# Conversion steps, warming matmuls, the order list of the attention rounds, and GpSimd for one part of a token mix

## The chip, the cores and the metric

The kernel runs on one core of a Trainium2 chip. TensorE (PE) multiplies matrices, VectorE (DVE), ScalarE (ACT) and GpSimd (POOL) work on tiles, and SyncE (SP) issues the DMAs. Each engine takes its instructions from a queue of its own, in order, and semaphores make one engine wait for another. The metric is the device time of one execution in microseconds (us); less is better.

## The reference, cut to what matters

Three blocks stand behind each other. Only their shapes matter here: two batches, 12 heads, 448 tokens, 64 numbers per head, 768 = 12 x 64 model columns, 1024 hidden columns.

```python
scores = scale * np.matmul(q, k.transpose(0, 1, 3, 2))       # causal mask, then softmax
x = softmax(scores) @ v                                      # heads joined: 768 columns
xk = mu_k * x + (1.0 - mu_k) * x_prev                        # x_prev: the token before
xr = mu_r * x + (1.0 - mu_r) * x_prev
x2 = sigmoid(xr @ w_r) * (np.maximum(xk @ w_k, 0.0) ** 2 @ w_v)
h = np.maximum(x2 @ w_in, 0.0)
out = (h * sigmoid(conv(h, conv_w)) @ w_out)
```

The weights arrive as 64-bit floating point numbers, so the kernel has to turn them into 32-bit ones itself.

## The kernel before

**Attention.** There are 12 jobs, one for each batch and pair of heads, numbered 0 to 11. The loop at L450 runs rounds i = -1 to 14. In each round the table `ORDER` (L426) names the operations of several jobs in the order in which every engine gets them: `n` is the next job (its transposes `kqT`, their copies `kqH` and `kqL`, its first scores `sc`), `c` the job of this round (more scores, `red` for the row maximum on DVE, `exp` on ACT), `l` the last one (`norm` on GpSimd, transposes `T` on PE, copies `C`), `p` the one before (`V`, the product with v on PE, and `out`), `a` the one before that (`mixP`, `mixD`, `mixH`, `mixL`). Within the rounds PE, ACT, DVE and GpSimd follow this order by hand; around them a scheduler has placed the instructions, so some matmuls of the next block already stand between the last rounds' work.

**Token mixes.** For each 128 columns c and batch b a mix has four steps: scale the token before (`mix_p`), add the scaled token (`mix_d`, L343, DVE), write the rounded high part (`mix_h`), and write the rest (`mix_l`, a subtraction at L78). Kind 1 makes xr inside the rounds with GpSimd for all but `mix_d`. Kind 0 makes xk behind the rounds: scaling and high part on ACT, `mix_d` and the subtraction on DVE.

**Matrix products.** Every fp32 product is made of three matmuls (`mm3`, L63 to 66): high by high (L64), high by low (L65), low by high (L66). The blocks are called by their banks: `pr` = xr @ w_r (6 weight slices, 216 matmuls), `pk` (8 slices), `pv`, `ph` and `pout`.

**Weight conversion.** A slice of weights (`wr0` to `wr5`, then `wk0` and so on) goes through seven steps, each taken by one call of `step()` (L407): one `Abs` on ACT (L100), four operations on DVE (L102, L104, L106, L108), the high part on ACT (`wr0hl`, L74), the low part on DVE (`wr0hl`, L78). In the rounds `c.w.0` to `c.w.2` take three steps per job from job 4 on, 24 in all; two more follow behind the loop (L465). `take()` finishes what is missing when a product needs the slice.

**Warming matmuls.** `keep_warm(n)` (L443) issues n matmuls whose result nobody reads: 12 ahead of everything and three behind every `kqT`, `sc` and `T` of the rounds i = -1, 0 and 1, in all 69.

Of the kernel before, what the change touches and what calls it, by code (L numbers as in the profile page):

```python
# [19 lines left out]
def kernel(  # L20
# [39 lines left out]
    def f32(ap):  # L60
        return ap.bitcast(F32)
# [49 lines left out]
    def load(w, m, name, rows):  # L111

        if rows:
            kt, n = 1, w.shape[1]
            src = w[m * P:(m + 1) * P, :].rearrange("p (k f) -> p k f", k=1)
        else:
            kt, n = w.shape[0] // P, P
            src = w[:, m * P:(m + 1) * P].rearrange("(k p) f -> p k f", p=P)
        raw = wp.tile([P, NF * P], I64, tag="wraw", name=f"{name}{m}raw")

        in_order(
            nc.sync.dma_start(out=raw[:, :kt * n].rearrange("p (k f) -> p k f", k=kt), in_=src)
        )
        return raw, kt * n, f"{name}{m}"
# [82 lines left out]
    class Job:  # L207
# [4 lines left out]
            self.done = 0  # L212

        def load(self, first=False):
            for src, n in ((k, "k"), (q, "q"), (v, "v")):
                t = rawp.tile([CP, NQ, 2, D], F32, tag=n, name=f"r{n}_{self.n}", bufs=4 if n == "v" else 2)
                for j in range(2):
                    dma = nc.sync.dma_start(
                        out=t[:, :, j],
                        in_=src[self.b, 2 * self.hp + j].rearrange("(c p) d -> p c d", p=CP),  # L220
                    )
                    if first:
                        tc.keep_in_program_order(dma)
                self.raw[n] = t
# [33 lines left out]
        def red(self, c, j):  # L258

            w, i = (c + 1) * CP, 2 * c + j  # L260
            self.s[c, j] = s_sb = sp.tile([CP, S], F32, tag="s", name=f"s_{self.n}_{i}", bufs=3)
            nc.vector.tensor_tensor_reduce(  # L262
                s_sb[:, :w], self.scs[c][j][:CP, :w], maskw[:, S - w:], -SCALE, 3e38,
                ALU.add, ALU.min, self.st[:, 0, i:i + 1],
            )

        def exp(self, c, j):
            w, i = (c + 1) * CP, 2 * c + j
            self.p[j, c] = p = sp.tile([CP, w], F32, tag=f"p{c}{j}", name=f"p_{self.n}_{i}", bufs=2)
# [54 lines left out]
        def mixL(self):  # L324
            mix_l(1, xr[self.hp], self.b, self.hp)

        def w(self, _):
            if self.i >= 4:
                step()

    ms = {}
# [14 lines left out]
        split_h("p" if kind else "s", dst[:, 0, TOK[b]], ms[kind, b, c])  # L346

    def mix_l(kind, dst, b, c):
        split_l("p" if kind else "v", dst[:, 1, TOK[b]], ms[kind, b, c], dst[:, 0, TOK[b]])

    def mix(kind, dst, b, c):
        mix_p(kind, b, c)
        mix_d(kind, b, c)
        mix_h(kind, dst, b, c)
        mix_l(kind, dst, b, c)

    TOK = [slice(b * S, (b + 1) * S) for b in range(B)]
# [61 lines left out]
    def take():
# [4 lines left out]


    ORDER = """  # L426
        c.w.0 c.exp.0.1 l.rec.2.4 l.norm.1.1 p.T.3 c.sc.3 p.C.1 p.C.0 c.exp.0.0 a.mixP p.T.2 l.norm.1.0
        c.red.1.1 n.kqT.q c.red.1.0 p.C.3 c.w.1 a.mixD n.kqT.k c.sc.2 c.red.3.0 l.norm.3.1 c.exp.1.1
        c.red.3.1 p.C.2 p.V.0 l.norm.2.0 n.kqH.q n.kqH.k n.kqL.q p.V.2 c.exp.1.0 l.norm.2.1 l.norm.3.0
        c.exp.3.0 p.V.3 n.kqL.k p.V.1 c.exp.3.1 c.red.2.1 l.norm.0.0 l.T.4 n.sc.0 c.red.2.0 c.rec.0.2 n.sc.1  # L430
        c.w.2 c.exp.2.1 a.mixH a.mixL l.T.1 p.out l.T.0 c.norm.0.1 l.C.4 n.red.0.1 c.exp.2.0 n.red.0.0
    """
    ROUNDS_AGO = {"n": -1, "c": 0, "l": 1, "p": 2, "a": 3}
    order = [x.split(".") for x in ORDER.split()]
# [8 lines left out]
    def keep_warm(n):  # L443
        for _ in range(n):
            nc.tensor.matmul(warm[:, :P], ident, ident, start=True, stop=True)  # L445

    keep_warm(12)
    ET = mybir.EngineType
    with tc.manual_schedule(engines={ET.PE, ET.Activation, ET.DVE, ET.Pool}):
        for i in range(-1, B * NPAIR + 3):  # L450
            if 2 <= i + 2 < B * NPAIR:
                jobs.append(Job((i + 2) // NPAIR, (i + 2) % NPAIR))
                jobs[-1].load()
            if i in (0, 1, 2):
# [12 lines left out]
    actx.close()
    ring[:] = ["sc", "sc", "tr", "sc", "sc", "tr", "tr", "po"]
# [28 lines left out]
    for e in range(NE):  # L497
# [15 lines left out]
    for f in range(NF):  # L513
# [4 lines left out]
        for b, ph in enumerate(token_mm(f"ph{f}", w, x2, f == 0)):  # L518
# [3 lines left out]
            a = mixp.tile([P, S], F32, tag="m", name=f"cv{f}_{b}")  # L522
# [21 lines left out]
    for o0 in range(0, len(outs), 6):  # L544
# [46 lines left out]
```

## Time and profile before

| what | us |
|---|---|
| median of 3 runs (403.45 to 404.49) | 404.1 |
| the profiled execution | 406.98 |
| its span, first to last instruction | 405.1 |
| PE busy in the span | 394.0 |
| DVE busy | 301.8 |
| ACT busy | 235.9 |
| GpSimd busy | 120.1 |

The profile gives busy time of each engine, the groups of instructions by line, who waited for whom, the chain of work that ended last, and the instructions in order of time. The span runs through the rounds to about 131.5 us (the last `V`), through `pr` to 164.0 us, and then through `pk`, `pv`, `ph` and `pout`. A matmul's shown duration contains its way through the array, so the rate is read from one start to the next. An fp32 matmul of the rounds stands as two records.

### The profile page before, as it was taken

The numbers are of one execution on the slowest core, as the hardware profiler recorded it, in microseconds if no ns is written. First come the engines' busy times: TensorE is split into PE (matmuls) and PEld (weight loads), VectorE is DVE, ScalarE is ACT, GpSimd is POOL, SyncE is SP. The second block draws the span as 40 slices with busy tenths as digits, with TensorE's granted clock in tenths as the row PEclk, the third lists the DMA queues.
The fourth block names the chain that finished last, engine by engine and source line by source line (L and its number), as shares of the span: only waits on it lengthen the run. The fifth ranks groups of instructions, "written<-read, shape, count | busy, mean of one in ns | idle before, by whom it ended". The sixth has DMA issues, their size and how long they took to land.

```text
span 405.1 us, 6662 instructions
## 1 busy us (share of the span) xinstructions
PE 394.0 (97%) x2372; PEld 342.6 (85%) x2372; DVE 301.8 (75%) x622; ACT 235.9 (58%) x510; POOL 120.1 (30%) x165
## 2 busy tenths in 40 slices
PE   7999999999999899999999999999999999999996
PEld 7887766665677789999999999999999999999995
DVE  1557999999921899889789999987799999930000
ACT  2658989998911986488667854544455555423110
POOL 1135999999981200000000000000035234320000
PEclk9999999999999999999999999999999999999999
DMA  7523573553020024544544553442422220003111
GB/s 165 112 48 85 142 182 89 151 147 101 2 79 0 0 79 134 178 139 158 172 151 162 181 172 115 155 155 79 155 79 78 78 80 0 2 0 138 39 58 41
DMA packets 60158, 41.37 MB, mean 102 GB/s; under 512 B 34232, under 2 KB 59100, under 8 KB 60124
## 3 DMA queue, kind: packets, MB, share of 16 engines
q1 hardware_dynamic: 60124, 40.93, 33.7%
q8 instruction: 19, 0.31, 0.3%
q14 instruction: 15, 0.12, 0.1%
HBM read 38.17 MB, written 2.75 MB: 101 GB/s over the span
## 4 chain that ended last, share of the span: by engine, by line
PE 85%; DVE 6%; POOL 5%; issue 2%; ACT 2%; ACTq 0%; POOLq 0%
PE ph L64 5%; PE pv L65 5%; PE pv L64 5%; PE pk L65 5%; PE pk L64 5%; PE ph L66 5%; PE ph L65 5%; PE pk L66 5%; PE pv L66 5%; PE warm L445 5%; PE pout L65 5%; PE pout L66 5%; PE pout L64 5%; PE pp L290 4%; PE sc L251 4%; PE pr L64 3%
## 5 line engine op out<-in xcount | busy, mean ns | idle before, releaser
L529 POOL TENSOR_TENSOR cv<-cv,hT 128x448 f32<-128x448 f32 x16 | 24.7, 1550 | 196.8 <-ACT cv L528 196.8
L282 POOL TENSOR_SCALAR p<-p,st 112x112 f32<-112x112 f32 (+3 forms) x96 | 58.3, 626 | 29.4 <-ACT p L270 16.6
L270 ACT ACTIVATE p<-s,st 112x112 f32<-112x112 f32 (+3 forms) x96 | 50.2, 528 | 11.2 <-DVE st L262 7.4
L262 DVE CUSTOM_DVE_ANT_0 s<-sc,maskw 112x112 f32<-112x112 f32 (+3 forms) x96 | 38.8, 440 | 3.9 <-PE sc L251 3.5
L290 PEld LDWEIGHTS pp<-ident,p 112*112 112x112 f32 x240 | 23.3, 134 | 13.4 <-POOL p L282 5.6
L290 PE MATMUL pp<-ident,p 112*112 112x112 f32 x240 | 31.7, 267 | 2.0 <-POOL p L282 1.5
L251 PE MATMUL sc<-kT,qT 64*112 64x112 f32 (+3 forms) x288 | 30.6, 324 | 0.4 <-DVE kT L78 0.4
L556 ACT ACTIVATE osb<-pout 128x384 f32<-128x384 f32 x14 | 6.8, 492 | 35.3 <-PE pout L66 35.3
L307 PE MATMUL po<-pt,rv 112*64 112x448 f32 (+3 forms) x192 | 25.7, 407 | 0.0
L251 PEld LDWEIGHTS sc<-kT,qT 64*112 64x112 f32 x288 | 19.0, 172 | 6.6 <-DVE kT L78 0.5
L298 DVE COPY pt<-pp 112x448 f32<-112x448 f32 x24 | 14.8, 617 | 13.1 <-PE pp L290 13.1
L445 PE MATMUL warm<-ident 128*128 128x128 f32 x138 | 22.4, 310 | 1.8 <-POOL ident masks.py:199 1.8
L298 ACT COPY pt<-pp 112x448 f32<-112x448 f32 x36 | 17.9, 527 | 9.7 <-PE pp L290 9.5
L445 PEld LDWEIGHTS warm<-ident 128*128 128x128 f32 x138 | 19.4, 215 | 3.4 <-POOL ident masks.py:199 1.8
L343 DVE SCALAR_TENSOR_TENSOR m<-xT,mu,m 128x448 f32<-128x448 f32 x24 | 16.5, 703 | 6.2 <-POOL m L337 6.2
L307 PEld LDWEIGHTS po<-pt,rv 112*64 112x64 f32 x192 | 11.4, 136 | 9.6 <-issue 8.4
L270 ACT ACTIVATION_READ_ACCUMULATOR p<-s,st 112x1 f32 x96 | 18.8, 195 | 0.0
L78 POOL TENSOR_TENSOR xr<-m,xr 128x448 fp32r<-128x448 f32 x12 | 17.9, 1492 | 1.0
L74 ACT ACTIVATE g<-cv 128x448 fp32r<-128x448 f32 x16 | 9.3, 579 | 13.7 <-POOL cv L529 13.2
L528 ACT ACTIVATE cv<-cv 128x448 f32<-128x448 f32 x16 | 9.2, 578 | 13.4 <-DVE cv L525 13.4
L65 PE MATMUL pout<-wo_t,g 128*128 128x384 f32 x49 | 16.5, 336 | 0.0
L66 PE MATMUL pout<-wo_t,g 128*128 128x384 f32 x49 | 16.5, 336 | 0.0
(501 smaller groups left out, 1212.4 us busy)
## 6 DMA issues: line engine op xcount, KB each, us to landing
rk<-in_k_dram SPq DMA_DIRECT2D x24, 112.0 KB, 2.6
rq<-in_q_dram SPq DMA_DIRECT2D x24, 112.0 KB, 2.5
rv<-in_v_dram SPq DMA_DIRECT2D x24, 112.0 KB, 2.4
out_dram<-osb SPq DMA_DIRECT2D x14, 192.0 KB, 1.9
wv0raw<-in_moe_w_v_dram SPq DMA_DIRECT2D x1, 1024.0 KB
wv1raw<-in_moe_w_v_dram SPq DMA_DIRECT2D x1, 1024.0 KB, 4.9
wv2raw<-in_moe_w_v_dram SPq DMA_DIRECT2D x1, 1024.0 KB
wv3raw<-in_moe_w_v_dram SPq DMA_DIRECT2D x1, 1024.0 KB, 4.9
```

What stands on the lines that cost most here:

```text
L64: nc.tensor.matmul(ps_out, lh, rh, start=first, stop=False)
L65: nc.tensor.matmul(ps_out, lh, rl, start=False, stop=False)
L66: nc.tensor.matmul(ps_out, ll, rh, start=False, stop=last)
L251: nc.tensor.matmul(scs[j][:CP, :w], qT[r, 1 if pi == 2 else 0, c * CP:(c + 1) * CP], kT[r, 1 if pi == 1 else 0, :w], start=pi == 0, stop=p ...
L262: nc.vector.tensor_tensor_reduce(s_sb[:, :w], self.scs[c][j][:CP, :w], maskw[:, S - w:], -SCALE, 3e38, ALU.add, ALU.min, self.st[:, 0, i:i ...
L270: nc.scalar.activation(p, self.s[c, j][:, :w], AF.Exp, bias=self.st[:, 0, i:i + 1], scale=-1.0, accum_out=self.st[:, 1, i:i + 1],)
L282: nc.gpsimd.tensor_scalar(self.p[j, c], self.p[j, c], self.st[:, 2, i:i + 1], 1.0, ALU.mult, ALU.mult)
L290: nc.tensor.transpose(pp[:CP, i * CP:(i + 1) * CP], self.p[j, c][:, kc * CP:(kc + 1) * CP], ident[:CP, :CP])
L298: (nc.vector.tensor_copy if bi in TURN_V else nc.scalar.copy)(pt, self.pp[bi][:CP, :S])
L307: nc.tensor.matmul(self.po[j * D:(j + 1) * D, c0 * CP:S], self.raw["v"][:, kc, j], pt[:, off:off + S - c0 * CP], start=kc == 0, stop=self. ...
L445: nc.tensor.matmul(warm[:, :P], ident, ident, start=True, stop=True)
L529: nc.gpsimd.tensor_tensor(a, a, hc, ALU.mult)
```

## The change

- The steps of weight conversion in a round go from three to two: `c.w.0` and, for the job of the round before, `l.w.1`, and job 11 takes none. That is 14 steps in the rounds. Behind the loop one slice is finished or made whole (`convert_next()`) and five more steps follow. So at the end the same slices stand at the same step, but only `wr0` and `wr1` are converted inside the rounds, where it had been three slices and three steps of the fourth.
- The warming matmuls ahead of everything go from 12 to 7, and those in round 1 (27) are gone. 37 are left of 69.
- Each job loads q before k.
- The subtraction of the xk mixes (`mix_l` of kind 0, 12 instructions) goes from DVE to GpSimd.
- `ORDER` is new: the same operations of a job, with `mixP` one round earlier (at the end of the round in which `out` is written) and all transposes and copies of a job in one round or at the start of the next.

```diff
@@ Job.load
-            for src, n in ((k, "k"), (q, "q"), (v, "v")):
+            for src, n in ((q, "q"), (k, "k"), (v, "v")):
@@ Job.w
-            if self.i >= 4:
+            if 4 <= self.i < 11:
                 step()
@@ mix_l
-        split_l("p" if kind else "v", dst[:, 1, TOK[b]], ms[kind, b, c], dst[:, 0, TOK[b]])
+        split_l("p", dst[:, 1, TOK[b]], ms[kind, b, c], dst[:, 0, TOK[b]])
@@ ORDER (first line of five)
-        c.w.0 c.exp.0.1 l.rec.2.4 l.norm.1.1 p.T.3 c.sc.3 p.C.1 p.C.0 c.exp.0.0 a.mixP p.T.2 l.norm.1.0
+        p.C.0 l.rec.2.4 l.norm.1.0 n.kqT.q c.exp.0.1 p.C.2 l.norm.0.0 c.exp.0.0 c.sc.1 n.kqH.q c.red.3.0
@@ warming
-    keep_warm(12)
+    keep_warm(7)
-                    if i < 2 and what in ("kqT", "sc", "T"):
+                    if i < 1 and what in ("kqT", "sc", "T"):
                         keep_warm(3)
@@ behind the loop
-    for _ in range(2):
+
+    convert_next()
+    for _ in range(5):
         step()
```

**PE at the start of round 1.** `warm` is the warming matmul, `ptrq` and `ptrk` the transposes of q and k of job 2, `sc_1` scores of job 1. Before:

```order
L251 MATMUL sc_1_3_1_326<-kT_1_258,qT_1_256 112x448
L445 MATMUL warm<-ident 128x128 x3
L231 MATMUL ptrq_2_341<-ident,rq_2_192 128x112 x4
L445 MATMUL warm<-ident 128x128 x3
L231 MATMUL ptrk_2_351<-ident,rk_2_189 128x112 x4
L445 MATMUL warm<-ident 128x128 x3
L251 MATMUL sc_1_2_0_359<-kT_1_258,qT_1_256 112x336
```

Now:

```order
L251 MATMUL sc_1_3_1_283<-kT_1_240,qT_1_222 112x448
L445 MATMUL warm<-ident 128x128 x3
L231 MATMUL ptrq_2_318<-ident,rq_2_184 128x112 x4
L251 MATMUL sc_1_1_0_328<-kT_1_240,qT_1_222 112x224
L251 MATMUL sc_1_1_1_329<-kT_1_240,qT_1_222 112x224
```

Behind the last warming matmuls of round 0 the transposes and scores now follow each other directly, and another slice of scores comes first.

**DVE at the end of attention.** `m_1_4` and `m_1_5` are the last `mix_d` of xr, `pt_5` copies of job 11, `m_0_0` and on the `mix_d` of xk, `wr2c` to `wr4c` weight slices in conversion. Before:

```order
L298 COPY pt_5_3_2037<-pp_5_3_2021 112x448
L343 SCALAR_TENSOR_TENSOR m_1_4_2030<-xT,mu,m_1_4_2030 128x448
L343 SCALAR_TENSOR_TENSOR m_1_5_2054<-xT,mu,m_1_5_2054 128x448
L343 SCALAR_TENSOR_TENSOR m_0_0_2122<-xT,mu,m_0_0_2122 128x448
L343 SCALAR_TENSOR_TENSOR m_1_0_2127<-xT,mu,m_1_0_2127 128x448
L78 TENSOR_TENSOR xk_2070<-m_0_0_2122,xk_2070 128x448
L78 TENSOR_TENSOR xk_2070<-m_1_0_2127,xk_2070 128x448
L343 SCALAR_TENSOR_TENSOR m_0_1_2175<-xT,mu,m_0_1_2175 128x448
```

Now:

```order
L298 COPY pt_5_4_1974<-pp_5_4_1966 112x448
L343 SCALAR_TENSOR_TENSOR m_1_4_1976<-xT,mu,m_1_4_1976 128x448
L343 SCALAR_TENSOR_TENSOR m_1_5_2005<-xT,mu,m_1_5_2005 128x448
L102 TENSOR_SCALAR wr2c<-wr2c 128x768
L104 TENSOR_SCALAR wr2c<-wr2c 128x768
L343 SCALAR_TENSOR_TENSOR m_0_0_2090<-xT,mu,m_0_0_2090 128x448
L106 SCALAR_TENSOR_TENSOR wr2c<-wr2raw,wr2c 128x768
L343 SCALAR_TENSOR_TENSOR m_1_0_2095<-xT,mu,m_1_0_2095 128x448
L108 SCALAR_TENSOR_TENSOR wr2c<-wr2raw,wr2c 128x768
L343 SCALAR_TENSOR_TENSOR m_0_1_2143<-xT,mu,m_0_1_2143 128x448
L343 SCALAR_TENSOR_TENSOR m_1_1_2148<-xT,mu,m_1_1_2148 128x448
L78 TENSOR_TENSOR wr2hl<-wr2c,wr2hl 128x768
```

The whole conversion of `wr2` now stands behind `m_1_5`, the last step that waits for the last `out`; the subtractions of xk have left this queue.

**PE behind the last `V`.** `po_5` is the product with v of job 11, `pr_0` and `pr_1` the banks of the two batches, `xr_88` and `xr_89` the last two column groups of xr. Before:

```order
L307 MATMUL po_5_2042<-pt_5_3_2037,rv_5_1556 64x336
L66 MATMUL pr_0_2135<-xr_88,wr1hl 128x448
L64 MATMUL pr_1_2083<-xr_88,wr0hl 128x448
L64 MATMUL pr_0_2135<-xr_89,wr1hl 128x448
L65 MATMUL pr_0_2135<-xr_89,wr1hl 128x448
L66 MATMUL pr_0_2135<-xr_89,wr1hl 128x448
L64 MATMUL pr_1_2136<-xr_88,wr1hl 128x448
L64 MATMUL pr_0_2196<-xr_88,wr2hl 128x448
```

Now:

```order
L307 MATMUL po_5_1993<-pt_5_3_1972,rv_5_1530 64x112
L65 MATMUL pr_1_2051<-xr_88,wr0hl 128x448
L66 MATMUL pr_1_2051<-xr_88,wr0hl 128x448
L65 MATMUL pr_1_2104<-xr_88,wr1hl 128x448
L66 MATMUL pr_1_2104<-xr_88,wr1hl 128x448
L64 MATMUL pr_1_2051<-xr_89,wr0hl 128x448
L64 MATMUL pr_1_2104<-xr_89,wr1hl 128x448
L65 MATMUL pr_1_2051<-xr_89,wr0hl 128x448
L66 MATMUL pr_1_2051<-xr_89,wr0hl 128x448
L65 MATMUL pr_1_2104<-xr_89,wr1hl 128x448
L66 MATMUL pr_1_2104<-xr_89,wr1hl 128x448
L64 MATMUL pr_0_2164<-xr_84,wr2hl 128x448
```

Before, 40 matmuls with `wr0` to `wr2` stand between the last `V` and the first one with `wr3`. Now there are ten with `wr0` and `wr1`, and then `wr2` is wanted; 62 matmuls of `pr` stand ahead of the last `V`'s end, where it had been 68.

## Rows read from the trace of the kernel before

**Rows 1.** By stretch: length, busy time and (xinstructions) per engine, PEclk, DMA share, GB/s

```profile
1.77:7.05 5.28, 5.28 (x24) 5.28 (x25) 0.00 (x0) 0.24 (x1) 0.25 (x2) 1.00 0.89 202
22.08:33.67 11.59, 11.59 (x104) 10.17 (x103) 5.74 (x27) 6.30 (x20) 3.54 (x9) 1.00 0.18 42
33.67:55.82 22.15, 22.15 (x207) 15.54 (x206) 21.13 (x74) 20.69 (x66) 18.93 (x30) 1.00 0.60 147
55.82:97.04 41.22, 38.73 (x343) 26.28 (x342) 40.41 (x139) 37.80 (x115) 40.33 (x54) 1.00 0.48 122
97.04:109.19 12.15, 11.13 (x97) 6.98 (x96) 12.05 (x44) 12.13 (x39) 12.07 (x19) 1.00 0.21 67
109.19:131.52 22.33, 22.33 (x139) 17.75 (x137) 5.63 (x11) 4.15 (x10) 12.66 (x17) 1.00 0.11 36
131.52:163.97 32.45, 30.89 (x149) 27.67 (x150) 29.99 (x45) 25.37 (x45) 2.98 (x3) 1.00 0.23 73
163.97:401.30 237.33, 237.23 (x1201) 220.54 (x1199) 177.86 (x252) 119.72 (x194) 25.84 (x22) 1.00 0.33 108
```

**Rows 2.** Chain that ended last, round 1: start us, us, what

```profile
21.38 0.87 PE warm L445 x6
...
31.07 0.68 PE warm L445 x6
```

**Rows 3.** Instructions by time at the head: start, us, engine, line, what, [idle before]

```profile
1.77 5.48 PE L445 MATMUL warm<-ident 128*128 128x128 f32 x24 [1.77 <-POOL ident masks.py:199]
7.47 0.85 PE L445 MATMUL warm<-ident 128*128 128x128 f32 x6
...
8.15 0.55 PE L231 MATMUL ptrk<-ident,rk 112*128 112x112 f32 x4
...
9.99 0.41 PE L251 MATMUL sc<-kT,qT 64*112 64x112 f32 x4 [0.35 <-DVE kT L78]
```

**Rows 4.** By time, GpSimd subtracting xr, once beside DVE's conversion, once alone

```profile
101.80 2.04 POOL L78 TENSOR_TENSOR xr<-m,xr 128x448 fp32r<-128x448 f32 x1
...
118.52 1.15 POOL L78 TENSOR_TENSOR xr<-m,xr 128x448 fp32r<-128x448 f32 x1
```

**Rows 5.** By time, DVE's conversion steps between 55.82 and 109.19 us, three of 14

```profile
56.87 0.95 DVE L108 SCALAR_TENSOR_TENSOR wr0c<-wr0raw,wr0c 128x768 int32<-128x768 int32 x1
...
101.89 0.93 DVE L78 TENSOR_TENSOR wr2hl<-wr2c,wr2hl 128x768 fp32r<-128x768 f32 x1
...
108.42 0.79 DVE L104 TENSOR_SCALAR wr3c<-wr3c 128x768 int32<-128x768 int32 x1
```

**Rows 6.** By time on PE, behind the last `V`

```profile
141.38 0.47 PE L64 MATMUL pr<-xr,wr3hl 128*128 128x448 f32 x1 [1.56 <-ACT wr3hl L74]
```

**Rows 7.** By time on DVE, behind the last `V`

```profile
132.88 2.18 DVE L343 SCALAR_TENSOR_TENSOR m<-xT,mu,m 128x448 f32<-128x448 f32 x3 [5.70 <-POOL m L337]
```

**Rows 8.** By time on DVE, in `pr`: starts give the pace of each step

```profile
139.87 0.55 DVE L102 TENSOR_SCALAR wr4c<-wr4c 128x768 f32<-128x768 f32 x1
140.34 0.61 DVE L78 TENSOR_TENSOR xk<-m,xk 128x448 fp32r<-128x448 f32 x1
140.87 0.55 DVE L104 TENSOR_SCALAR wr4c<-wr4c 128x768 int32<-128x768 int32 x1
141.36 0.96 DVE L78 TENSOR_TENSOR wr3hl<-wr3c,wr3hl 128x768 fp32r<-128x768 f32 x1
142.23 0.95 DVE L106 SCALAR_TENSOR_TENSOR wr4c<-wr4raw,wr4c 128x768 int32<-128x768 int32 x1
143.10 0.68 DVE L343 SCALAR_TENSOR_TENSOR m<-xT,mu,m 128x448 f32<-128x448 f32 x1
```

**Rows 9.** By time in `ph`, DVE's L525 without and with GpSimd's product L529 beside it

```profile
307.47 0.67 DVE L525 SCALAR_TENSOR_TENSOR cv<-hT,cw,cv 128x448 f32<-128x448 f32 x1
...
309.60 1.57 DVE L525 SCALAR_TENSOR_TENSOR cv<-hT,cw,cv 128x448 f32<-128x448 f32 x1
```

**Rows 10.** The same time on GpSimd

```profile
308.83 1.85 POOL L529 TENSOR_TENSOR cv<-cv,hT 128x448 f32<-128x448 f32 x1 [2.67 <-ACT cv L528]
```

More of the change, by code (lines that the diff above doesn't have):

```diff
@@ L426 @@
     ORDER = """
-        c.w.0 c.exp.0.1 l.rec.2.4 l.norm.1.1 p.T.3 c.sc.3 p.C.1 p.C.0 c.exp.0.0 a.mixP p.T.2 l.norm.1.0
[L428 to L431, printed above, removed]
+        p.C.0 l.rec.2.4 l.norm.1.0 n.kqT.q c.exp.0.1 p.C.2 l.norm.0.0 c.exp.0.0 c.sc.1 n.kqH.q c.red.3.0
+        n.kqT.k c.exp.3.0 a.mixD c.red.3.1 c.red.1.1 n.kqH.k l.norm.1.1 n.kqL.q c.exp.3.1 c.exp.1.1 p.V.0
+        l.norm.3.1 p.V.1 p.V.2 c.red.1.0 l.norm.2.1 p.V.3 c.exp.1.0 n.kqL.k l.norm.3.0 l.norm.2.0 c.sc.2
+        a.mixH p.out l.T.1 l.C.1 l.w.1 c.red.2.1 c.red.2.0 l.T.3 c.rec.0.2 l.T.4 c.exp.2.1 n.sc.0 a.mixL
+        l.C.3 l.C.4 p.mixP n.sc.3 c.norm.0.1 l.T.0 n.red.0.1 c.exp.2.0 n.red.0.0 c.w.0 l.T.2
     """
```

## The prediction

> **What bounds the kernel now.** I read the windows first, one per stage [rows 1]: a stage in which PE is busy for its whole length is bounded by PE, so only instructions taken out of PE's queue shorten it. From 163.97 us to the end PE is busy 237.23 of 237.33 us: nothing that DVE gains there moves the end, so of the xk edit only what happens before 163.97 counts. The tail of attention is full too (22.33 of 22.33), and in `pr` PE lacks 1.56 us, one wait for the high part of `wr3` [rows 6]. In the rounds there are three kinds. Round 1 (22.08 to 33.67) is full, 11.59 us, and much of that is warming. Rounds 2 to 4 take 22.15 us, 7.38 each, PE never idle: the floor of a round. Rounds 5 to 9 take 41.22 us, 8.24 each, PE lacks 2.49, and DVE (40.41) and GpSimd (40.33) are both busy to 98%: these rounds belong to the two together. Behind the last `V` DVE is busy 29.99 of 32.45 us, and GpSimd only 2.98.
>
> DVE and GpSimd are not independent. A subtraction of GpSimd takes 1.15 us alone and 2.04 beside a conversion step of DVE of 0.93 [rows 4, 5]: it is longer by that step's whole length. The other way round, in `ph`, a DVE step of 0.67 us takes 1.57 while GpSimd multiplies [rows 9, 10]: held for 0.9. There are 16 such pairs in `ph`, of which this one is shown; the holds lie between 0.73 and 0.96 us, 0.8 in the mean.
>
> **The change part by part.** All of it is against the profiled 406.98 us, which stands 2.9 above the median; differences are carried to the median.
>
> *Head.* Twelve warming matmuls (24 records) fill PE from 1.77 to 7.05 us, 5.28 / 24 = 0.22 a record [rows 1]; the six from 7.47 to 8.15 take 0.113 each [rows 3]. So the early ones go at half the pace, the lower level of the clock, though its column shows 1.00 there too [rows 1]. Ten records fewer free 10 x 0.22 = 2.2 us of PE. But the first scores wait for `kT` at 9.99 after all [rows 3]: behind PE stands the chain of load, transposes and copies, and what follows at the low level is slower. q comes first now, which suits the transposes. I take half, −1.1 (−0.6 if more runs at the low level, −1.5 if the copies follow at once).
>
> *Round 1.* Nine blocks of three warming matmuls stand in its chain, 0.68 to 0.87 us each [rows 2], 6.87 together, and PE is the bound, so nearly all of it goes, which leaves 4.7. ACT's 6.30 us of work there [rows 1] would be next: if it ends the round, 11.59 − 6.30 = 5.3, and with some waiting 4. Less work is in round 1 than in a full round, and part of ACT's can run into round 2. I take −6.4, bounds −4 and −6.9.
>
> *Rounds 5 to 11.* Between 55.82 and 109.19 there are 14 conversion steps of DVE before [rows 5]. Counted from the list it will be ten: 14 calls are two slices with five DVE operations each. Four at about 0.85 us are 3.4 us off the pair that bounds these rounds: −3.4. If the new list makes new waits or the steps lay in gaps, 0; if every round falls to the floor, 5 x (8.24 − 7.38) = 4.3, and the 1.02 that PE lacks in 97.04 to 109.19 [rows 1], −5.3.
>
> *The tail.* 62 instead of 68 matmuls of `pr` fill PE there. What isn't done before the last `V` is done behind it, so PE's sum is unchanged, and I count nothing; T, the end of the last `V`, is 131.52.
>
> *Behind the last V.* Here the change costs. Before, 40 matmuls with finished slices (8.3 us at 0.207, 30.89 for 149 [rows 1]) cover the end of `wr3`, and PE waits 1.56. Now ten are left, 2.1 us, and the whole of `wr2` stands in DVE's queue behind `m_1_5`, which waits for GpSimd's `m` of the last `out`: DVE idles 5.70 us ahead of it and starts at 132.88, T+1.36 [rows 7]. So it is done at T+1.96. Steps go by the starts of neighbours in `pr` [rows 8]: 0.47 and 0.49 for L102 and L104, 0.87 for L106 and L78, and the same for L108, 0.60 for a `mix_d`. Up to `wr2`'s low part there are the five steps (3.57) and four `mix_d` (2.40): T+7.9. PE has been dry since about T+2.1; with L64 and L65, which want the high part only, it does a few more and then waits. Up to `wr3`'s low part there are five steps more, three of `wr4` (1.83) and four `mix_d`: 7.8, T+15.7. `wr2`'s 36 matmuls (7.5 us) end about then, so DVE's next slice is what PE waits for.
>
> Meanwhile GpSimd subtracts, once for xr and then behind each `mix_d` of xk, in the same stretch in which DVE works without a pause. Before `wr2`'s low part four such subtractions fall, before `wr3`'s seven, and up to nine when counted generously. At 0.8 us a hold [rows 9, 10], `wr2` is ready at T+11.1 and `wr3` at 15.7 + 7 x 0.8 = T+21.3. Behind it 104 matmuls stand (three slices of 36, less the four that want the high part alone), 21.5 us at 0.207, the same pace. So `pr` ends at T+42.8, where it had been T+32.45 [rows 1]: +10.4. With no hold at all it is 15.7 + 21.5 − 32.45 = +4.8; with nine holds +12.0, and with seven for GpSimd's whole 1.15 us [rows 4] +12.9. What the move takes off DVE, the subtractions of 0.53 [rows 8], is already left out of these sums. I take the 0.8 because it is measured with a two-input step of DVE beside a two-input step of GpSimd, which is what stands here.
>
> *Sum.* −1.1 − 6.4 − 3.4 + 10.4 = −0.5. The profiled run would take 406.5, the median **403.6 us**. The first three terms lie between −4.6 and −13.7, the last between +4.8 and +12.9, so the outer ends are −8.9 and +8.3.
>
> **The rivals.**
>
> *B: GpSimd's subtractions fall into gaps.* For: DVE waits for ACT's high parts here and there, and a hold in a wait costs nothing. Against: in `ph` sixteen of the holds were real. One or two holds in seven stay: the last term is +6, and the time 404.1 − 1.1 − 6.4 − 3.4 + 6 = 399.2. If the rounds reach their floor as well, 397.3.
>
> *C: the other side.* Place: the DVE queue behind `m_1_5`. If every GpSimd subtraction keeps DVE out for its own length of 1.15 [rows 4], the last term is 12.9 and the time 404.1 + 2.0 = 406.1. It decides from where the last term exceeds 10.9 + 1.2 (the 0.3%), 12.1. For: the queue has no slack there, and the hold that [rows 9, 10] show, 0.9, is already above the mean of 0.8. Against: that mean. The rule of the holder in the Trainium skill (SBUF — State Buffer, Who interferes with whom), by which the one that comes first keeps the pair for his whole instruction, would give these 1.15 whenever GpSimd comes first; the trace agrees for GpSimd's side, 2.04 against 1.15 [rows 4], and shows 0.9 on DVE's.
>
> *D: the clock.* Behind the head PE's pace stays at the higher level, with a granted clock of 1.00, and its longest wait that the rows show is 1.56 us [rows 1, 6]. Now it waits several us between T+2 and T+11, and the warming of round 1 is gone too. If the clock falls to 1.2 GHz and stays there as long as in the head, 5.28 us at half the pace [rows 1], half of that is lost: 2.6 us, 406.2. The Trainium skill (TensorE: Matmul & The Clock Gate, Part 1) says that throttled is the default state, that activity releases it and that idling brings it back; the head agrees with the release (0.22, then 0.113), and no run here shows a return.
>
> *E: the list does not do what it says.* The rounds gain nothing, since the new order has a wait of its own: the third term is 0 and the time 407.0. For: only its rows can show it. Against: transposes and copies of a job stand close together in it and its steps on DVE are fewer.
>
> **How the numbers follow.** Forecast 0.45 (own range 401.5 to 405.5), B 0.25, C 0.12, D 0.10, E 0.08. The range of 8 in 10 takes in B and all of the slower cases: 399.0 to 408.0. What a measurement can tell is 0.3%, 1.2 us. Of the forecast's share I put 0.16 below 402.9, 0.26 between and 0.03 above 405.3; B is faster, C, D and E slower: faster 0.41, same 0.26, slower 0.33.
>
> **What would show it.** Head and round 1: 74 records of warming in the group of L445; round 1 between 4.7 and 6 us. Rounds 5 to 11: starts of `ptrq` 7.5 to 7.8 us apart, DVE below 98%; 8.2 would be E. Behind the last `V`: a wait of PE for `wr2hl` of L78 some 5 us long, another of about as much for `wr3hl`, GpSimd's L78 for xk twelve times, each above 1.15 us where DVE is busy, and DVE's L106, L108 stretched to some 1.7; `pr` ends about 163. The clock column at 1.00 there speaks against D, below it for D. The prediction is wrong at its largest term if PE doesn't wait for `wr2hl`, or if DVE's steps stay at their 0.95 beside GpSimd's. It is wrong at the second if round 1 stays near 8 us because ACT or the row maxima end it.

## The result and the profile after

The changed kernel takes 407.06 us (median of 12 runs, 405.12 to 409.18), the kernel before, beside it, 404.19: the ratio is 1.0069, interval 1.0048 to 1.0090. Run again beside other kernels it came out at 406.0 against 404.43, 1.0024 (0.9992 to 1.0056). So it is slower by 0.9% at most, and by the second interval perhaps not at all. The forecast was 403.6 us, 0.5 below the kernel before: the range holds the result, the direction is wrong. The ratios leave out slow executions, among them one of 627.54 us (xk back on DVE) and one of 1333.64 us (the kernel before).

The profiled execution of the changed kernel took 408.7 us, its span 406.9 (before: 406.98 and 405.1). The windows of the changed kernel, cut at the same events as in [rows 1] (length, then busy time and instructions of PE, weight loads, DVE, ACT, GpSimd, then granted clock, DMA share, GB/s):

```profile
1.77:4.92 3.15, 3.15 (x14) 3.15 (x15) 0.00 (x0) 0.24 (x1) 0.25 (x2) 1.00 0.85 193
19.86:25.86 6.00, 5.99 (x56) 4.47 (x55) 5.63 (x23) 5.33 (x17) 3.84 (x8) 1.00 0.34 78
25.86:48.09 22.23, 22.23 (x204) 15.93 (x205) 19.93 (x76) 20.59 (x67) 17.14 (x31) 1.00 0.60 148
48.09:85.06 36.97, 36.97 (x343) 26.49 (x342) 36.63 (x135) 35.41 (x114) 35.95 (x56) 1.00 0.46 115
85.06:97.24 12.18, 12.18 (x107) 8.32 (x106) 12.08 (x40) 11.76 (x38) 12.03 (x18) 1.00 0.21 67
97.24:117.95 20.71, 20.71 (x128) 16.07 (x125) 5.35 (x14) 4.81 (x12) 10.22 (x16) 1.00 0.00 1
117.95:165.81 47.86, 37.47 (x157) 31.95 (x156) 44.03 (x46) 29.47 (x50) 19.94 (x15) 0.86 0.31 99
165.81:403.10 237.29, 237.23 (x1201) 220.54 (x1199) 176.04 (x248) 117.37 (x191) 23.97 (x22) 1.00 0.32 104
```

Round 1 is down from 11.59 to 6.00 us, rounds 5 to 9 from 41.22 to 36.97 with PE never idle, the tail from 22.33 to 20.71. With the head's 2.2 (round 1 starts at 19.86 instead of 22.08) the last `V` ends at 117.95 instead of 131.45, 13.5 us earlier. All that and more goes in the one stretch behind it: 47.86 us, where it had been 32.52 (131.45 to 163.97). There PE is busy 37.47 us only, GpSimd 19.94 instead of 2.98, and the granted clock is 0.86. From `pk` on nothing differs between these two profiles (237.29 against 237.33).

What PE waited for in the changed kernel (us in total, times, longest):

```profile
PE pr L64 <- ACT wr2hl L74: 3.6, 1, 3.6
PE pr L66 <- DVE wr3hl L78: 3.2, 1, 3.2
PE pr L64 <- POOL xr L70: 2.0, 1, 2.0
...
PE pr L64 <- ACT wr3hl L74: 0.8, 1, 0.8
PE pr L65 <- POOL xr L78: 0.7, 1, 0.7
```

The five add up to 10.3 us, all behind the last `V`; the kernel before had the one of 1.56 there [rows 6]. Now PE in time there, [idle before] at the end:

```profile
127.13 0.74 PE L64 MATMUL pr<-xr,wr2hl 128*128 128x448 f32 x1 [3.65 <-ACT wr2hl L74]
...
141.52 0.74 PE L66 MATMUL pr<-xr,wr3hl 128*128 128x448 f32 x1 [3.16 <-DVE wr3hl L78]
142.06 0.57 PE L64 MATMUL pr<-xr,wr3hl 128*128 128x448 f32 x1
142.43 0.57 PE L65 MATMUL pr<-xr,wr3hl 128*128 128x448 f32 x1
...
147.82 0.37 PE L64 MATMUL pr<-xr,wr3hl 128*128 128x448 f32 x1
148.03 0.37 PE L65 MATMUL pr<-xr,wr3hl 128*128 128x448 f32 x1
```

Behind each of the two long waits the matmuls start 0.37 us apart and later 0.207: the lower level of the clock, then the higher one. The windows show the granted clock of the same time:

```profile
124.00:127.00 3.00, 0.00 (x0) 0.00 (x0) 3.00 (x3) 2.66 (x7) 1.83 (x2) 0.50 0.00 0
133.00:135.00 2.00, 2.00 (x12) 1.85 (x11) 2.00 (x3) 0.61 (x2) 1.18 (x1) 1.00 0.00 0
143.00:145.00 2.00, 2.00 (x7) 1.78 (x6) 2.00 (x2) 2.00 (x4) 1.19 (x1) 0.50 0.00 0
149.00:151.00 2.00, 2.00 (x12) 1.81 (x11) 2.00 (x2) 0.41 (x1) 0.74 (x1) 1.00 0.00 0
```

Between 124 and 127 us PE did nothing and was granted 0.50; at 133 it had 1.00, at 143, behind the next wait, 0.50 again, at 149 1.00. The Trainium skill (TensorE: Matmul & The Clock Gate, Part 1) says that throttled is the default and that idling brings it back; this trace agrees, twice.

And DVE and GpSimd in time, where [rows 8] shows DVE's steps undisturbed:

```profile
119.38 0.68 DVE L343 SCALAR_TENSOR_TENSOR m<-xT,mu,m 128x448 f32<-128x448 f32 x1 [8.05 <-POOL m L337]
119.98 0.55 DVE L102 TENSOR_SCALAR wr2c<-wr2c 128x768 f32<-128x768 f32 x1
...
128.04 0.95 DVE L78 TENSOR_TENSOR wr2hl<-wr2c,wr2hl 128x768 fp32r<-128x768 f32 x1
128.91 1.49 DVE L102 TENSOR_SCALAR wr3c<-wr3c 128x768 f32<-128x768 f32 x1
...
133.22 1.51 DVE L102 TENSOR_SCALAR wr4c<-wr4c 128x768 f32<-128x768 f32 x1
...
139.59 1.88 DVE L78 TENSOR_TENSOR wr3hl<-wr3c,wr3hl 128x768 fp32r<-128x768 f32 x1
...
148.65 1.91 DVE L78 TENSOR_TENSOR wr4hl<-wr4c,wr4hl 128x768 fp32r<-128x768 f32 x1
```

```profile
128.44 2.98 POOL L78 TENSOR_TENSOR xk<-m,xk 128x448 fp32r<-128x448 f32 x2 [1.40 <-ACT xk L74]
133.12 1.18 POOL L78 TENSOR_TENSOR xk<-m,xk 128x448 fp32r<-128x448 f32 x1 [1.71 <-ACT xk L74]
...
138.89 3.58 POOL L78 TENSOR_TENSOR xk<-m,xk 128x448 fp32r<-128x448 f32 x2 [1.70 <-ACT xk L74]
```

L102 takes 0.55 us alone and 1.49 and 1.51 where GpSimd's subtraction has begun before it; L78 takes 1.88 instead of 0.95. With T for the end of the last `V`, here 117.95, `wr2`'s low part is done at 128.91, T+11.0, `wr3`'s at 141.47, T+23.5, and `wr4`'s at 150.56, T+32.6. Why all of `wr2` stands there is in ACT's rows:

```profile
118.07 0.54 ACT L313 COPY xT<-po 128x448 f32<-128x448 f32 x1 [5.89 <-PE po L307]
118.50 0.90 ACT L100 ACTIVATE wr2c<-wr2raw 128x768 f32<-128x768 f32 x1
```

The first step of `wr2` is an ACT operation that is kept in the order of the program, and so behind the copy of the last `out`, for which ACT waited 5.89 us.

### The profile page after: what moved, and what is told of

Read it like the earlier page. It is cut to its first block, busy times and chain, and to the rows that moved or that the text cites. A ratio compares the mean times of both kernels' runs of the same rounds, so it can differ in the third digit from the quotient of the medians.

```text
span 406.9 us, 6520 instructions
## 1 busy us (share of the span) xinstructions
PE 390.5 (96%) x2308; PEld 339.5 (83%) x2308; DVE 307.4 (76%) x610; ACT 233.8 (57%) x510; POOL 126.1 (31%) x177
## 4 chain that ended last, share of the span: by engine, by line
PE 93%; DVE 5%; issue 1%; ACT 0%; POOL 0%; ACTq 0%; POOLq 0%
PE sc L251 7%; PE pp L290 6%; PE po L307 6%; PE ph L64 5%; PE pv L65 5%; PE pv L64 5%; PE pk L65 5%; PE pk L64 5%; PE ph L66 5%; PE ph L65 5%; PE pv L66 5%; PE pk L66 5%; PE pout L65 5%; PE pout L66 5%; PE pout L64 5%; PE pr L64 3%
## 5 line engine op out<-in xcount | busy, mean ns | idle before, releaser
L531 POOL TENSOR_TENSOR cv<-cv,hT 128x448 f32<-128x448 f32 x16 | 22.8, 1423 | 183.2 <-ACT cv L530 183.2
L282 POOL TENSOR_SCALAR p<-p,st 112x112 f32<-112x112 f32 (+1 forms) x96 | 52.4, 564 | 22.0 <-DVE st L278 19.4
L290 PE MATMUL pp<-ident,p 112*112 112x112 f32 x240 | 28.3, 264 | 0.0
L343 DVE SCALAR_TENSOR_TENSOR m<-xT,mu,m 128x448 f32<-128x448 f32 x24 | 20.5, 862 | 8.1 <-POOL m L337 8.1
L298 ACT COPY pt<-pp 112x448 f32<-112x448 f32 x36 | 19.2, 535 | 7.7 <-PE pp L290 7.6
L307 PEld LDWEIGHTS po<-pt,rv 112*64 112x64 f32 x192 | 12.5, 136 | 11.7 <-issue 4.7
L78 POOL TENSOR_TENSOR xk<-m,xk 128x448 fp32r<-128x448 f32 x12 | 17.2, 1440 | 14.8 <-ACT xk L74 14.8
L298 DVE COPY pt<-pp 112x448 f32<-112x448 f32 x24 | 13.5, 605 | 8.7 <-PE pp L290 8.7
L270 ACT ACTIVATION_READ_ACCUMULATOR p<-s,st 112x1 f32 x96 | 19.4, 202 | 0.0
L78 POOL TENSOR_TENSOR xr<-m,xr 128x448 fp32r<-128x448 f32 x12 | 16.3, 1358 | 1.0
L65 PE MATMUL pout<-wo_t,g 128*128 128x384 f32 x49 | 16.5, 336 | 0.0
L66 PE MATMUL pout<-wo_t,g 128*128 128x384 f32 x49 | 16.5, 336 | 0.0
L64 PE MATMUL pout<-wo_t,g 128*128 128x384 f32 x49 | 16.4, 335 | 0.0
L74 ACT ACTIVATE g<-cv 128x448 fp32r<-128x448 f32 x16 | 9.2, 576 | 10.3 <-POOL cv L531 10.2
```

The source lines that it names most:

```text
L64: nc.tensor.matmul(ps_out, lh, rh, start=first, stop=False)
L65: nc.tensor.matmul(ps_out, lh, rl, start=False, stop=False)
L66: nc.tensor.matmul(ps_out, ll, rh, start=False, stop=last)
L270: nc.scalar.activation(p, self.s[c, j][:, :w], AF.Exp, bias=self.st[:, 0, i:i + 1], scale=-1.0, accum_out=self.st[:, 1, i:i + 1],)
L282: nc.gpsimd.tensor_scalar(self.p[j, c], self.p[j, c], self.st[:, 2, i:i + 1], 1.0, ALU.mult, ALU.mult)
L290: nc.tensor.transpose(pp[:CP, i * CP:(i + 1) * CP], self.p[j, c][:, kc * CP:(kc + 1) * CP], ident[:CP, :CP])
```

## The experiments

The kernels ran in three groups, with the kernel before beside each group (403.08, 403.49 and 404.43 us). Times of different groups are compared by their ratios to it, and places in the program by the stages of the profiles.

### The warming matmuls alone

```diff
-    keep_warm(12)
+    keep_warm(7)
-                    if i < 2 and what in ("kqT", "sc", "T"):
+                    if i < 1 and what in ("kqT", "sc", "T"):
```

> The kernel before with the change's two edits to the warming matmuls alone (7 instead of 12 ahead, none in round 1). Theory: head and round 1 are bounded by PE, so the 2.2 and 5.6 us that the changed kernel shows there come through to the end: ptrq of round 2 near 26 instead of 33.7 us, every later stage as before, about 396.4 us. Rival: the rounds behind, which belong to DVE and GpSimd, or the clock, give part of it back: 399 to 403 us.

Measured: 396.19 us, ratio 0.9809 (0.9754 to 0.9864): 6.9 us less by the medians and 7.7 by the ratio, near the 7.8 expected. Its windows of round 1 and of rounds 5 to 9:

```profile
19.67:26.84 7.17, 6.53 (x57) 4.74 (x56) 6.41 (x30) 6.50 (x22) 4.71 (x10) 1.00 0.29 65
48.98:90.09 41.11, 38.74 (x342) 26.29 (x341) 40.30 (x139) 37.64 (x114) 40.28 (x53) 1.00 0.49 124
```

The gain is not given back: rounds 5 to 9 take what they took (41.22 in [rows 1]). And with the old list and k before q round 1 takes 7.17 us, not 6.00, so 1.2 us of round 1 belong to the new list, or to q's place, which this run leaves as it was. This one edit alone gains, where the whole change loses.

### xk back on DVE

```diff
-        split_l("p", dst[:, 1, TOK[b]], ms[kind, b, c], dst[:, 0, TOK[b]])
+        split_l("p" if kind else "v", dst[:, 1, TOK[b]], ms[kind, b, c], dst[:, 0, TOK[b]])
```

> The changed kernel with the subtractions of xk back on DVE. Theory that GpSimd's subtractions hold DVE: wr3's low part comes 15.7 + 7 x 0.53 = 19.4 us behind the last V instead of 23.5, so pr ends 4.1 us earlier, about 403.0 us; if the wait of 3.2 us goes with it and the clock doesn't fall a second time, 400.1 us. Rival, that the order alone (wr2 behind m_1_5) is the whole cost: DVE has seven operations more and no hold less, 407 us or more.

Measured: 399.42 us, ratio 0.9883 (0.9817 to 0.9950), 5.7 to 7.5 us below the changed kernel, by its second ratio or its first. From the last `V` to `pk`, and the waits:

```profile
117.06:159.33 42.27, 36.08 (x157) 31.27 (x155) 36.97 (x56) 28.35 (x48) 2.76 (x3) 0.88 0.30 93
```

```profile
PE pr L64 <- ACT wr2hl L74: 2.4, 1, 2.4
...
PE pr L66 <- DVE wr3hl L78: 1.1, 1, 1.1
```

DVE has more to do and is ready earlier: `wr3`'s low part comes at T+21.0 (19.4 was expected) instead of T+23.5, and the wait for it shrinks from 3.2 to 1.1 us. The rival (the place of `wr2` is the whole cost) is out. It is half right, though: 42.27 is still 9.8 us above the 32.52 of before, and that is the place, as the run with two steps and the old list shows further down (42.74).

### The twelve steps put into the tail

```diff
+            if i == 11:
+                convert_next()
+            if i == 12:
+                for _ in range(5):
+                    step()
-    convert_next()
-    for _ in range(5):
-        step()
```

> The changed kernel with the twelve steps that stand behind the loop put into it: wr2's seven behind round 11, five of wr3 behind round 12, where DVE and ACT stand idle. Theory that the place of wr2's conversion is the cost behind the last V: the waits for wr2 and wr3 (3.6, 0.8 and 3.2 us) and the fall of the clock go, pr ends some 33 us behind the last V instead of 47.9, about 392 to 394 us. Rival, that the end of attention is lengthened by the same steps: the last V ends up to 5 us later than 118 us, 397 to 399 us.

Measured: 401.8 us, ratio 0.9956 (0.9922 to 0.9989). Neither number came: the waits for `wr2` and the long one for `wr3` are gone, but the wait moved on by one slice, to `wr4`, and the granted clock was 0.50 from 140 to 150 us, in and behind that one:

```profile
PE pr L64 <- ACT wr4hl L74: 4.7, 1, 4.7
PE pr L66 <- DVE wr4hl L78: 2.5, 1, 2.5
```

The last `V` ends 3.9 us later than in the run with xk on DVE (120.98 against 117.06), and that costs little, since 20 matmuls with `wr2` (4.1 us) now lie ahead of it.

### Filling the wait for wr3

Twelve repeats of `wr3`'s first matmul, which the true first one overwrites.

```diff
+        for _ in range(fill):
+            nc.tensor.matmul(out_[0], w[0][:, 0, 0:P], x[0][:, 0, 0:S], start=True, stop=True)
```

> The changed kernel with twelve needless repeats (2.5 us of PE) of the first matmul with wr3, overwritten afterwards, in the wait for wr3's low part. Theory that idling drops the clock there: it stays at 1.00, the 17 matmuls at 0.374 us go at 0.207, pr ends 2.9 us earlier, about 404.2 us. Rival, that the clock falls for another reason or that DVE holds the end anyway: 407 us or up to 0.5 more.

Measured: 405.9 us, ratio 1.0062 (1.0030 to 1.0094): as the changed kernel. The place in question, PE's time and the granted clock, and then what PE waited for:

```profile
143.00:145.00 2.00, 2.00 (x12) 1.85 (x11) 2.00 (x3) 1.59 (x3) 1.15 (x1) 1.00 0.35 47
...
147.00:149.00 2.00, 0.97 (x5) 0.56 (x3) 2.00 (x2) 0.00 (x0) 2.00 (x2) 1.00 0.05 17
```

```profile
PE pr L66 <- DVE wr4hl L78: 1.9, 1, 1.9
...
PE pr L66 <- DVE wr3hl L78: 0.8, 1, 0.8
```

Both theories were half right. With the wait filled PE keeps its clock: 1.00 where it had been 0.50. But it then arrives at `wr4` too early, and waits 1.9 us for DVE. From the last `V` to `pk` this kernel takes 47.02 us; the changed kernel in its second run, whose matmuls had the same pace (`pk` in 58.37 us in both), takes 46.59. `wr4`'s low part comes at T+32.7 here, and at T+32.6 and T+32.7 in the two profiles of the changed kernel. Some 70 matmuls stand behind it, 14 us, so DVE alone puts the end of `pr` at about T+46.7, whatever the clock does for `wr3`. The fall of the clock is there, and it hides in the lateness of DVE.

### Three steps with the new list

```diff
-            if 4 <= self.i < 11:
+            if self.i >= 4:
-        ... l.norm.3.0 l.norm.2.0 c.sc.2
+        ... l.norm.3.0 l.norm.2.0 c.w.2 c.sc.2
-    convert_next()
-    for _ in range(5):
+    for _ in range(2):
```

> The changed kernel with a third step of conversion in every round (24 in the rounds, two behind the loop, as before the change), all the rest of the change kept. It tells apart what brought rounds 5 to 9 from 41.2 to 37.0 us. If the two steps did it, these rounds are back near 41 us; if the new list did it, they stay near 37. Behind the last V wr2 is finished, but GpSimd still subtracts xk, so the wait moves on to wr4 as in the run with the steps in the tail, some 5 to 7 us. Against the kernel before: 3 us less in the first case, 7 to 8 us less in the second.

Measured: 411.23 us, ratio 1.0200 (1.0151 to 1.0249). Neither gain came. Rounds 5 to 9:

```profile
46.83:91.73 44.90, 42.67 (x343) 28.95 (x341) 41.91 (x137) 38.18 (x116) 35.88 (x58) 0.92 0.45 115
56.05:66.57 10.52, 10.52 (x70) 6.80 (x69) 8.88 (x31) 8.40 (x24) 6.83 (x12) 0.68 0.44 110
```

They are slower than with the old list and as many steps (41.22). In these rounds PE waits 2.1 us for DVE's row maxima ahead of `sc`, in three places, the longest 1.2 us. The second line is one of the five rounds: 10.52 us long, with PE busy throughout and a granted clock of 0.68. The other four had 1.00 and took 8.15 to 9.22 us, so the clock is only a part of the loss. So the list isn't good by itself; where I put the third step in it may have a part in this, which one run cannot tell.

### The tail's steps and xk on DVE

Both edits together:

```diff
+            if i == 11:
+                convert_next()
...
-        split_l("p", dst[:, 1, TOK[b]], ms[kind, b, c], dst[:, 0, TOK[b]])
+        split_l("p" if kind else "v", dst[:, 1, TOK[b]], ms[kind, b, c], dst[:, 0, TOK[b]])
```

> The kernel with the twelve steps in the tail, and the subtractions of xk back on DVE. Theory that GpSimd's holds, not the place of wr2, moved the wait on to wr4 (4.7 and 2.5 us): both go, the clock stays up, some 8 us less than with the steps in the tail alone, 9 to 10 us less than the kernel before. Rival, that DVE is as late with seven subtractions more: the wait for wr4 stays, at most 3 us less than with the steps in the tail alone.

Measured: 396.81 us, ratio 0.9840 (0.9781 to 0.9899), 6 to 7 us below the kernel before instead of 9 to 10. The waits for `wr4` go from 4.7 and 2.5 us to 2.4 and 0.6, and the last `V` to `pk` from 40.31 to 36.38. GpSimd's holds moved the larger part of the wait; a smaller part stays, and the clock doesn't stay up as expected (0.91 between the last `V` and `pk`).

### xk on GpSimd in the kernel before

```diff
-        split_l("p" if kind else "v", dst[:, 1, TOK[b]], ms[kind, b, c], dst[:, 0, TOK[b]])
+        split_l("p", dst[:, 1, TOK[b]], ms[kind, b, c], dst[:, 0, TOK[b]])
```

> The kernel before with the xk subtractions on GpSimd and nothing else. Theory: although the 40 matmuls with finished slices are there, DVE is held by GpSimd in every slice that follows, wr4 comes too late for PE and PE waits 4 to 7 us: 4 to 7 us slower than the kernel before, all of it between the last V and the end of pr. Rival, that the stock of 40 matmuls covers it: no change within 1 us.

Measured: 412.46 us, ratio 1.0220 (1.0182 to 1.0258), some 9 us more. Behind the last `V`, and the waits there:

```profile
132.72:169.55 36.83, 31.16 (x150) 27.58 (x149) 32.47 (x33) 24.85 (x44) 19.32 (x15) 1.00 0.20 65
```

```profile
PE pr L64 <- ACT wr3hl L74: 2.0, 1, 2.0
...
PE pr L66 <- DVE wr4hl L78: 1.5, 1, 1.5
PE pr L66 <- DVE wr5hl L78: 1.4, 1, 1.4
```

The rival (40 matmuls cover it) is out: this stretch is 4.3 us longer, with three slices late. The clock stayed at 1.00. The expectation put the whole loss here, and that was wrong: 4.3 us of the 9 are here. In this trace rounds 5 to 9 also take 43.20 us instead of 41.22, though the edit changes nothing in them. That, and the rest, isn't explained.

### Three steps, the new list, xk on DVE

```diff
-            if 4 <= self.i < 11:
+            if self.i >= 4:
-        ... l.norm.3.0 l.norm.2.0 c.sc.2
+        ... l.norm.3.0 l.norm.2.0 c.w.2 c.sc.2
-        split_l("p", dst[:, 1, TOK[b]], ms[kind, b, c], dst[:, 0, TOK[b]])
+        split_l("p" if kind else "v", dst[:, 1, TOK[b]], ms[kind, b, c], dst[:, 0, TOK[b]])
-    convert_next()
-    for _ in range(5):
+    for _ in range(2):
```

> The new list, the warming matmuls and q's place of the change, but three steps per round and xk on DVE as before the change. If the list alone frees the rounds, 8 + 4 us less than the kernel before and a little more from the tail, about 390 us; if the two steps did it, 8 us less, about 395 to 396 us.

Measured: 405.35 us, ratio 1.0026 (0.9991 to 1.0061). Rounds 5 to 9 take 44.17 us, so neither number came: as with three steps above, PE waits for the row maxima (3.2 us in these rounds) and the granted clock is below 1.00 (0.96). Against that run the edit of xk is worth 6 to 7 us once more, 4.8 of them between the last `V` and `pk` (38.53 and 33.69 us).

### Two steps with the old list

```diff
-            if self.i >= 4:
+            if 4 <= self.i < 11:
-        c.w.2 c.exp.2.1
+        c.exp.2.1
-    for _ in range(2):
+    convert_next()
+    for _ in range(5):
```

> The kernel before with two steps of conversion per round and seven plus five steps behind the loop, as in the change; list, warming and xk on DVE as before. If four DVE steps fewer are what freed rounds 5 to 9, they take 37 to 38 us here too, with the old list; if the new list has a part, they stay near 39 to 41. Behind the last V wr2 comes as late as in the changed kernel with xk on DVE (42 us to the end of pr instead of 32.5), so the whole is some 4 to 6 us slower than the kernel before in the first case and 8 to 10 us in the second.

Measured: 407.82 us, ratio 1.0100 (1.0066 to 1.0134). Rounds 5 to 9, and the stretch behind the last `V`:

```profile
55.65:94.18 38.53, 38.00 (x343) 26.09 (x341) 37.81 (x133) 35.98 (x112) 37.70 (x55) 1.00 0.51 133
125.42:168.16 42.74, 36.05 (x163) 31.64 (x161) 39.39 (x58) 29.78 (x49) 2.83 (x3) 0.92 0.32 103
```

The rounds lie between the two numbers. Of the 4.25 us that they gained in the changed kernel, 2.7 come with the two steps alone, and the last 1.6 with the list. The 42.74 behind the last `V`, without any xk on GpSimd, is the price of the place of `wr2`: 10.2 us above 32.52.

### The old list with all else

The change's warming and steps, the twelve steps in the tail and xk on DVE, with the old list and k before q.

```diff
-        c.w.2 c.exp.2.1
+        c.exp.2.1
-    keep_warm(12)
+    keep_warm(7)
...
+            if i == 11:
+                convert_next()
...
```

> The old list with two steps per round, seven and 36 warming matmuls... that is the change's warming, xk on DVE, and the twelve steps in the tail: it differs from the kernel with the new list, tail steps and xk on DVE in the list and in the order of q and k alone. If the new list is worth something by itself (round 1 in 6.0 instead of 7.2 us, rounds 5 to 9 in 37.0), this one is 1 to 4 us slower than that kernel (396.8 beside 403.5 before); if only the number of steps counts, within 1 us of it.

Measured: 402.82 us, ratio 0.9918 (0.9874 to 0.9962), against 0.9840 for its counterpart with the new list. By that the list is worth about 0.8%, 3 us, once two steps go with it, but the two intervals overlap and the runs lie from 398 to 404.5 us. The profiles say more: in both `pk` takes 59.52 us, and it starts at 161.63 us here and at 156.62 there, 5.0 us earlier. Of these round 1 has 1.2 (7.16 and 6.00) and rounds 5 to 9 have 1.5 (38.50 and 36.97). q's place is in the difference too.

### The xk mixes later

As the run with the tail's steps and xk on DVE, and:

```diff
-        for b in range(B):
-            mix(0, xk[e], b, e)
+        for c in ((), (), (), (0, 1), (2, 3), (4, 5))[e]:
+            for b in range(B):
+                mix(0, xk[c], b, c)
```

> The kernel with the twelve steps in the tail and xk on DVE, and the xk mixes issued with later slices (none with the first three, then two column groups each). Theory that DVE's queue ahead of wr4 is the rest of the wait (2.4 and 0.6 us, and the clock behind it): with one or two operations fewer ahead of wr4's low part the wait halves, 1 to 4 us less than with the mixes at their old place. Rival, that ACT's order around wr4's Abs decides: no change.

Measured: 393.91 us, ratio 0.9709 (0.9640 to 0.9778). It beats both kernels, by 10.5 and 12.1 us. In `pr` PE has one wait left, for `wr3`, and none for `wr4`. The stretch is below that of the kernel before, with 139 matmuls in it instead of 149:

```profile
120.75:152.54 31.79, 30.05 (x139) 26.79 (x138) 28.75 (x44) 24.67 (x44) 2.61 (x3) 0.95 0.20 62
```

```profile
PE pr L64 <- ACT wr3hl L74: 1.7, 1, 1.7
```

The granted clock still fell behind that wait: it was 0.71 from 130 to 135 us and 1.00 from 135 us on.

### The changed kernel again

Nothing is edited.

> The changed kernel itself, again, beside the others on one chip: 0.7% over the kernel before, PE waiting 3.6 us for wr2 and 3.2 us for wr3, and the clock down in both places.

Measured: 406.0 us, ratio 1.0024 (0.9992 to 1.0056), with waits of 2.9 us for `wr2` and 3.2 for `wr3`, and 0.85 as the granted clock of the 46.59 us between the last `V` and `pk`. The first ratio lay a little higher; the mechanism behind the last `V` is the same. One thing is new in this profile:

```profile
PE pout L64 <- ACT hT L523: 2.1, 1, 2.1
```

`pk` starts at 163.36 us, 0.6 earlier than in the profile of the kernel before, and `pout` then takes 62.50 us, where the run with xk back on DVE takes 58.49. So in this execution 4 us are lost at the far end, where the profiles of the two kernels above showed no difference.

## Why the prediction was wrong, point by point

| step | forecast, us | profiled, us |
|---|---|---|
| head | −1.1 | −2.2 |
| round 1 | −6.4 | −5.6 |
| rounds 5 to 11 | −3.4 | −4.2 |
| tail | 0 | −1.6 |
| behind the last `V` | +10.4 | +15.3 |
| sum | −0.5 | +1.7 (span: +1.8; medians: +2.9) |

**Head.** The first `ptrq` starts at 4.92 instead of 7.05, but in the profile of the result more warming and the first transposes then run at the slow pace, and the first scores that wait for `kT` come 0.86 us earlier than at 9.99 [rows 3]:

```profile
5.67 1.51 PE L445 MATMUL warm<-ident 128*128 128x128 f32 x6
...
9.13 0.41 PE L251 MATMUL sc<-kT,qT 64*112 64x112 f32 x4 [0.35 <-DVE kT L78]
```

That is inside the stated bounds. The other 1.36 us come from where the table cuts. Ahead of round 1's first `ptrq` a slice of scores (0.50) is missing, which the new list puts behind it, and three of the warming matmuls that are gone (0.87 [rows 2]) had stood there too. In the second profile of the changed kernel the same six records take 0.85 us and these scores come at 7.87, 2.1 us earlier, so there nothing was lost again and the bound of 1.5 was too narrow. Why the pace rises at different times isn't shown, and that the slow pace is the lower level of the clock isn't either, as the granted clock reads 1.00.

**Round 1.** Right in the mechanism. Of the nine blocks that I priced the first, 0.87 us at 21.38, stands ahead of 22.08, outside the 11.59 us that I took them from; and the new list, which I hadn't priced here, has 1.2 us of the gain, as the run with the warming alone shows. Head and round 1 together were forecast at −7.5 and came to −7.8.

**Rounds 5 to 11.** Right in place and near in size. Rounds 5 to 9 came to the floor, 7.39 each. The cause was given too simply: fewer DVE steps make 2.7 us of it, and the list adds 1.6, but only together with them; with three steps the same list costs 3.7 us (44.90 against 41.22), in part by one round at the lower clock.

**Tail.** I set it to zero because PE's sum is unchanged. Six matmuls fewer are 1.2 us there, and they are paid for in the next line; as a split between stages it was wrong, in the sum nearly right.

**Behind the last V.** The step that failed, by 4.9 us: the term of +10.4, in which DVE's holds were counted up to `wr3`'s low part and PE's 104 matmuls behind it were taken to run without a pause. The place, the order of the waits and the lateness of `wr2` were right: T+11.1 forecast, T+11.0 measured; waits of PE for `wr2`, then for `wr3`, and DVE's steps stretched beside GpSimd's. Three things were wrong.

*The holds.* I put seven at 0.8 us ahead of `wr3`, the mean of `ph`. (Eleven pairs inside `ph` show a hold, not sixteen; their mean is 0.8.) By the starts of DVE's steps there were eight, of 0.83 to 1.06 us, 0.92 in the mean; with smaller delays they make 23.5 − 15.7 = 7.8 us: T+23.5 instead of T+21.3. Rival C, in which each of seven holds lasts 1.15 us, gave T+23.8 and was nearer, but partly by luck: it has one hold too few, and none of the eight is as long. The Trainium skill (SBUF — State Buffer, Who interferes with whom) says that in some modes the first of the two keeps the shared pair to the end of his instruction; the L102 at 133.22 agrees: it starts 0.10 us into a subtraction of GpSimd (133.12, 1.18 long) and ends 0.43 behind that one's end, about its own length of 0.55.

*What follows.* The holds go on, and DVE takes 9.1 us more up to `wr4`'s low part, T+32.6, where T+21.3 with PE at its pace asks for it by about T+28.8. From there 68 matmuls at 0.207 are 14.1 us: T+46.7 of the 47.9 measured.

*The clock.* I made it a rival of its own, at 2.6 us and one in ten, when it follows here from the waits that my forecast itself contained. Seventeen matmuls at 0.374 instead of 0.207 are 2.8 us, but only some 1.2 of them come through, since PE would have waited for `wr4` otherwise.

The filled wait shows the same: the clock stays up, and the kernel gains nothing, because DVE is then late with `wr4`. What bounds the stretch is DVE's queue, and what made that too slow is shown by the edits: GpSimd's subtractions (4.3 us of this stretch in the kernel before, 4.3 to 5.6 in the changed one; the medians moved by more, 9 and 5.7 to 7.5) and the place of `wr2` behind the copy of the last `out` (42.74 against 32.52 us with two steps and xk on DVE). With the place alone mended the wait moves on to `wr4`; with both mended and the mixes later, it is gone.

**Where I chose wrongly.** My forecast carried GpSimd's interference as a few holds of one slice. It is one of every slice: the five DVE steps of a slice and its two `mix_d` are 4.8 us by [rows 8], two holds of 0.92 make that 6.6, against 7.5 that PE needs, so a queue that is late by several us gains less than 1 us a slice; measured it lost more, 9.1 us from `wr3`'s low part to `wr4`'s. And the run of the kernel before with this edit alone (+2.2%) says that the move is bad with or without the rest, which I had not asked of the profile: I had counted what it took off DVE (0.53 us each) as a gain of the sum, where each subtraction on GpSimd that meets a DVE step costs DVE some 0.92 in its place.

**The rivals.** B (the holds fall into gaps) is out. C's hold of 1.15 us was further from the measured 0.92 than my 0.8, though its time came nearer. D happened as a row but not as a cost of its own. E did not happen with two steps.

## What to carry to other kernels

In this kernel moving an operation from DVE to GpSimd freed DVE only where the two didn't meet: read the time of a DVE step beside a GpSimd step first, and if it is longer by more than the operation moved, leave it. Before work is pushed behind the last step of a stage, ask what its first operation is queued behind, on its own engine, and how many instructions the waiting engine has left. The changed kernel's two long waits of PE (3.65 and 3.16 us) were both followed by matmuls at the lower clock, so a forecast that contains such a wait should carry the clock in its sum, not as a rival; whether it costs anything depends on who is late next. And a wait of PE for one slice has to be followed through the slices behind it: here the next one, `wr4`, set the end.

## What the runs showed that I had not expected

The pace of PE's long blocks has two values at a granted clock of 1.00. `pk` takes 59.5 us in the profiles of the kernel before and of the changed one, and 58.37 in the second run of the changed kernel and in six others, 2% for the same instructions; two runs change between them (one has `pk` in 59.52 and `ph` in 58.37). Over the four blocks that is some 3.6 us, more than the change itself moves, so profiles of different runs were compared by stage here and not by span. What sets it stays open. PE's wait for `hT` ahead of `pout` stands only in profiles that have the faster pace in `pk` or `ph`, and only where GpSimd subtracts xk: five of those kernels' profiles have it (0.3 to 2.1 us), and none of the three with the faster pace and xk on DVE. Why isn't shown.

Rounds in which DVE and GpSimd are both full vary by 2 us in 41 with the same instructions in the same order (41.11, 41.22 and 43.20 us). And in the run with three steps in the new list the granted clock fell in one of the five rounds (0.68), though PE's waits in them for the row maxima were 1.2 us at most, where the kernel before kept 1.00 with waits of 0.6 and, with xk on GpSimd, of 1.1.
